# Attention outputs as positions by features turned by DMA in pairs, q and k of a block turned by one DMA, and groups of two

## The chip, the cores and the metric

The kernel runs on one core of one Trainium2 chip. The metric is device time in microseconds (us) of one execution. The core has a matrix engine (PE, with its weight loads listed as PEld), a vector engine (DVE), a scalar engine (ACT), GpSimd (POOL), and SyncE (SP), whose queue issues nearly all DMAs here; ACT's queue issues the stores of the output. Each engine works through its own queue in order.

## The reference, cut to what matters

Inputs q, k, v have shape 4 batches x 8 heads x 768 positions x 64 features. First comes linear attention with decay `lam` per head, in blocks along the positions:

```
intra = einsum('bhic,bhjc->bhij', qb, kb) * Dmask      # lam^(i-j) for j <= i
intra = einsum('bhij,bhjd->bhid', intra, vb)
inter = einsum('bhid,bhde->bhie', qb * lam_pow, kv_state)
out   = intra + inter
kv_state = lam_block * kv_state + einsum('bhsd,bhse->bhde', kb * rev_pow, vb)
```

The result, as 3072 tokens by 512 features (`x`), goes through two products: `h = x @ w_in` (512 x 2048), `g = h * sigmoid(h)`, and `g @ w_out` (2048 x 512), float32 at the end.

## The kernel before

Positions are taken 128 at a time: 24 blocks `u`, six for each batch (`blk` = 0 to 5 within a batch). Products are in bf16 with float32 sums in PSUM. For a block, `attention(u)` does this:

- q and k are loaded on SP's queue, scaled by powers of lam on DVE (`qs`, L325; `ks`, L390) and turned so that features lie on partitions. Blocks below `XB = 8` are turned on PE (`tr_ps`, L347, L398, L426). From block 8 on a DMA transpose on SP's queue does it: `kT` one block at a time (L409) and `qT` two blocks at a time (L337). For blocks 2 to 21 the positions of a pair of blocks are interleaved in q (`qf`, 512 KB for two blocks, L273); the four others (`plain`) load q on its own.
- `kTz` is k turned, put into a zero-padded tile by two copies (ACT or DVE, L230/L232).
- Scores `st_ps` (PE, L452, eight products), masked on DVE to `st_sb` (L461).
- The output `x_ps` (PE): eight products of `st_sb` with `vz`, v padded with zeros to two heads' width (L490), and for `blk > 0` four of the carried state `Xz` with q (L494). Here `vz` and `Xz` are the stationary operands, so the result lies as features x positions, 128 columns a product. ACT copies it into `xt` of the block's group (L230).
- The state: `d_ps` (PE, L521; L517 for the first blocks, where it is written in products of 64 columns), `y` on DVE, `Xz` and `Xf` on POOL (L235).

The blocks are put into groups for the two big products: `[0,1] [2,3] [4] [5] [6,7] [8,9] [10,11]` and then three groups of four. `first_product(g)` multiplies `w_in` (stationary) by the group's `xt` (moving, 128, 256 or 512 columns) into `h_ps` (L588); ACT makes `g` with SiLU (L597). `second_product(u)` multiplies `g` by `w_out`, 16 products of 512 columns for each block, into `o_ps` (L616; the last block's in halves, L655), which DVE copies to `o_sb` and ACT's queue stores.

Nothing waits on a clock. A planner (`Plan.run`) lists all steps with assumed costs, rings of buffers (`BUFS`) and priorities, and writes out each engine's instructions in the order that it finds. `pace(u)` and `at=` hold back steps of blocks 8 to 23 in this plan only: they set the order of the queues, not a wait on the chip. PE's queue so mixes the attention's short products with the big ones. In PE's order the attention of block 23 is followed by 76 products of L588 and 168 of L616, all with 512 columns, and the 32 of L655.

The order of both kernels' queues can be read without a run. Up to and with the 64 products of L588 for group `[6,7]` PE's two orders agree instruction by instruction; SP's agree up to the last load of `w_out`.

Of the kernel before, what the change touches and what calls it, by code (L numbers as in the profile page):

```python
# [7 lines left out]
F32 = mybir.dt.float32  # L8
# [92 lines left out]
def kernel(  # L101
# [10 lines left out]
    nc = tc.nc  # L112
# [10 lines left out]
    KO = DFF // 128  # L123
    HB = BLK // 2
    XB = 8
    WIDE = 4

    ctx.enter_context(tc.manual_schedule())
# [14 lines left out]
    def sb(o, name, shape, dtype, tag=None):  # L143
        return work.tile(shape, dtype, tag=tag or name, bufs=BUFS[tag or name], name=name)
# [80 lines left out]

    val = {}

    def copy(o, dst, src):
        if o["eng"] == "ACT":
            nc.scalar.activation(dst, src, AF.Copy)  # L230
        else:
            (nc.vector if o["eng"] == "DVE" else nc.gpsimd).tensor_copy(dst, src)  # L232
# [74 lines left out]
    def attention(u):  # L307
# [1 line left out]
        pr = at["v", u]  # L309


        if u in plain or u % 2 == 0:
            two = u not in plain
            lq = load["q", u]
            late = []
            if u >= 4:
                late = [plan.op({"NONE": 0.0}, [lq], lambda o: None, 0, after=2.0 if u >= 8 else 1.2, at=pace(u))]
# [13 lines left out]
            trs = []  # L331
            if u >= XB:
                n = len(halves)

                def fn(o):
                    val["qT", u] = sb(o, "qT", [128, 2, NP, BLK], BF16)
                    nc.sync.dma_start_transpose(  # L337
                        out=val["qT", u][:, 0:n].rearrange("p t a s -> p (t a) s"),
                        in_=val["qs", u][:, 0:n].rearrange("p t h d -> p (t h d)"))
                x = plan.op({"SP": 1.3 * n if n == 2 else 1.8}, [halves[-1]], fn, pr + 0.1, alloc=["qT"], frees=[(halves[0], "qs")])  # L340
                O["qT", u] = [x, plan.op({"NONE": 0.0}, [x], lambda o: None, 0, after=4.5)]
            for t in range(len(halves) if u < XB else 0):
# [9 lines left out]
            for t in range(len(halves) if u < XB else 0):  # L352
# [7 lines left out]
            if u < XB:  # L360
                O["qT", u] = evs
            if two:
                O["qT", u + 1] = O["qT", u]
        home = u if u in plain else u - u % 2

        def qT(p):
# [12 lines left out]
        if wide:  # L379
            def fn(o):  # L380
                val["ks", u] = kp[o["slots"]["kp"]]
                nc.vector.tensor_tensor(
                    val["ks", u].rearrange("p a b (c d) -> p a (b c) d", d=64)[:, :, 0:4:3, :],
                    val["kf", u].rearrange("p (a b) d -> p a b d", b=2),
                    lam_bwd.rearrange("p (a b) -> p a b", b=2)[:, :, :, None].to_broadcast([128, NP, 2, 64]),
                    op=AL.mult)
        else:
# [4 lines left out]
        ring_k = "kp" if wide else "ks"  # L392
        ks = plan.op({"DVE": 0.7}, [lk] + late, fn, pr, alloc=[ring_k], frees=[(lk, lk["tag"])])
        if wide:
            def fn(o):
                val["trk", u] = bank(o, "tr", [128, 2 * NP, BLK], BF16)
# [7 lines left out]
            kz = [plan.op({"ACT": 1.02, "DVE": 1.22}, [tk], fn, pr, alloc=["kTz"],  # L404
                          frees=[(tk, "bank"), (tk, "n_tr")])]
        elif u >= XB:
            def fn(o):
                val["kT", u] = sb(o, "kT", [128, NP, BLK], BF16)
                nc.sync.dma_start_transpose(  # L409
                    out=val["kT", u], in_=val["ks", u].rearrange("p h d -> p (h d)"))  # L410
            tk = plan.op({"SP": 1.8}, [ks], fn, pr, alloc=["kT"])
            landed = plan.op({"NONE": 0.0}, [tk], lambda o: None, 0, after=4.5)
            kz = []
            for hh in range(2):
                def fn(o, hh=hh):
                    if hh == 0:
                        val["kTz", u] = kTz[o["slots"]["kTz"]]
                    r = slice(64 * hh, 64 * hh + 64)
                    copy(o, val["kTz", u][r, :, hh, :], val["kT", u][r])
                kz.append(plan.op({"ACT": 0.59, "DVE": 0.35}, [tk, landed] + kz[:1], fn, pr,  # L420
                                  alloc=["kTz"] if hh == 0 else [], frees=[(tk, "kT")] if hh else []))
        else:
            def fn(o):
                val["trk", u] = bank(o, "tr", [128, NP, BLK], BF16)
# [57 lines left out]
        def fn(o):  # L482
# [4 lines left out]
            for p in range(NP):  # L487
# [7 lines left out]
        oo = plan.op({"PE": 0.0556 * (8 if blk == 0 else 12)}, masks + [vc] + prev_x + ([O["out", u - 1]] if u else []), fn, pr + 0.4,  # L495
                     alloc=["bank", "n_x"], frees=gives)
# [5 lines left out]
        O["xt", u] = plan.op({"ACT": 0.6, "DVE": 0.69}, [oo], fn, pr + 0.4, frees=[(oo, "bank"), (oo, "n_x")])  # L502

        last_st["frees"].append((kz[0], "kTz"))

# [5 lines left out]
        def fn(o):  # L511
            d = bank(o, "d", [128, NP, 64 if wide else 128], F32)
            val["d", u] = d
            for p in range(NP):
# [9 lines left out]
        dd = plan.op({"PE": 0.45 if wide else 0.225}, [ks, tk, vc], fn, pr + 0.35,  # L524
                     alloc=["bank", "n_d"], frees=[(ks, ring_k)])
        ys = []
        for hh in range(1 if wide else 2):
# [49 lines left out]
    def first_product(g):  # L577
# [4 lines left out]
        for m in range(KO // per):  # L582
            def fn(o, m=m):
                t = bank(o, "h", [128, per, nb * BLK], F32)
                val["h", g, m] = t
                for j in range(per):
                    for ko in range(KI):
                        nc.tensor.matmul(  # L588
                            t[:, j, :], lhsT=w_in_bf[:, ko, (m * per + j) * 128:(m * per + j + 1) * 128],
                            rhs=xts[g][:, ko, :], start=(ko == 0), stop=(ko == KI - 1))  # L590
# [138 lines left out]
```

## Time and profile before

| | us |
|---|---|
| median of 3 runs (lowest to highest) | 224.34 (224.01 to 224.50) |
| the profiled execution's own time | 223.49 |
| its span, first to last instruction | 221.8 |
| PE busy | 212.1 (96%) |
| PEld busy | 134.8 (61%) |
| DVE busy | 117.6 (53%) |
| ACT busy | 109.1 (49%) |
| POOL busy | 51.7 (23%) |
| SP's DMA queue (q1), packets' time as a share of 16 engines | 63.7%, 31.67 MB |
| ACT's DMA queue (q10) | 11.0%, 6.10 MB |

Busy times of different engines overlap. A matmul's duration in the profile holds the time that it spends in the array's pipeline; the next one starts well before it ends, so the distance from start to start tells what a product costs in a row of them. "x16" behind a piece is a count of instructions merged into it.

### The profile page before, as it was taken

To read this page: it belongs to the slowest core of one execution; us is meant where nothing else is said; L and a number is where in the kernel's file an instruction comes from. 1 tells how busy PE (TensorE), PEld (TensorE's weight loads), DVE (VectorE), ACT (ScalarE), POOL (GpSimd) and SP (SyncE) were. 2 spreads that over 40 slices of the span, in tenths; PEclk is the share of its full clock that TensorE was granted. 3 is DMA by queue.
4 is the path that set the end of the run, shared out by engine and by line. 5 is a ranking of instruction groups with operands and counts; after the bars stand their busy time and mean duration, and the time that the engine had idled before them with its cause. 6 is when DMAs were issued, how large, how long until landed. Compare 5 with 4: busy or idle time off the path is not lost.

```text
span 221.8 us, 4271 instructions
## 1 busy us (share of the span) xinstructions
PE 212.1 (96%) x1686; PEld 134.8 (61%) x1709; DVE 117.6 (53%) x198; ACT 109.1 (49%) x190; POOL 51.7 (23%) x71
## 2 busy tenths in 40 slices
PE   4889999999999999999999999999999999999994
PEld 1566699998745557978765656555554444444453
DVE  5676857878327786577788689753401120022121
ACT  5495488895712326785726773785351025500000
POOL 7364403035004051260444350442000000000000
PEclk9699999999999999999999999999999999999999
DMA  5999999999989979999999999910220422024332
GB/s 119 229 296 290 338 255 254 271 394 340 189 212 229 271 169 232 196 230 231 201 219 234 184 229 145 210 24 3 47 47 3 89 53 47 0 51 94 75 67 95
DMA packets 90243, 38.03 MB, mean 171 GB/s; under 512 B 72560, under 2 KB 83184, under 8 KB 90224
## 3 DMA queue, kind: packets, MB, share of 16 engines
q1 hardware_dynamic: 86448, 31.67, 63.7%
q10 hardware_dynamic: 3776, 6.10, 11.0%
q8 instruction: 13, 0.21, 0.4%
q14 instruction: 6, 0.05, 0.1%
HBM read 27.27 MB, written 6.29 MB: 151 GB/s over the span
## 4 chain that ended last, share of the span: by engine, by line
PE 87%; DMA 7%; DVE 2%; issue 1%; ACT 1%; SPq 1%; DVEq 0%
PE h_ps L588 37%; PE o_ps L616 36%; PE st_ps L452 4%; PE x_ps L490 4%; DMA wst<-in_moe_w_in_dram 4%; DMA qf<-in_q_dram 2%; PE x_ps L494 2%; PE d_ps L521 2%; PE o_ps L655 1%; DMA out_dram<-o_sb 1%; SPq L270 1%; PE tr_ps L347 1%; DVE w_in_bf L232 1%; DVE st_sb L461 1%; PE tr_ps L398 0%
## 5 line engine op out<-in xcount | busy, mean ns | idle before, releaser
L588 PE MATMUL h_ps<-xt,w_in_bf 128*128 128x256 bf16 (+2 forms) x634 | 89.9, 293 | 0.8 <-ACT xt L230 0.5
L616 PE MATMUL o_ps<-w_out_bf,g 128*128 128x512 bf16 x355 | 82.3, 379 | 0.7
L597 ACT ACTIVATE g<-h_ps 128x512 bf16<-128x512 f32 x96 | 56.5, 596 | 38.0 <-PE h_ps L588 22.3
L588 PEld LDWEIGHTS <-w_in_bf 128*128 128x128 bf16 x640 | 56.0, 98 | 23.1 <-PE x_ps L494 0.6
L616 PEld LDWEIGHTS <-g 128*128 128x128 bf16 x368 | 35.0, 98 | 37.6
L235 POOL TENSOR_TENSOR Xz<-y,lam_blk 64x256 bf16<-64x256 f32 x40 | 33.8, 845 | 99.2 <-DVE y L537 33.6
L232 DVE COPY o_sb<-o_ps 128x512 f32<-128x512 f32 (+2 forms) x24 | 15.9, 663 | 61.9 <-PE o_ps L616 58.8
L461 DVE TENSOR_TENSOR st_sb<-st_ps,mask 128x512 bf16<-128x512 f32 x48 | 32.0, 687 | 12.8 <-PE st_ps L452 12.6
L230 ACT ACTIVATE xt<-x_ps 128x512 bf16<-128x512 f32 x24 | 14.3, 595 | 26.1 <-PE x_ps L494 24.8
L325 DVE TENSOR_TENSOR qs<-qf,lam_fwd 128x512 bf16<-128x512 f32 x24 | 18.4, 780 | 3.5 <-DMA qf<-in_q_dram 3.4
L537 DVE TENSOR_TENSOR y<-d_ps,Xf 64x256 f32<-64x256 f32 (+1 forms) x29 | 12.2, 421 | 12.1 <-POOL Xf L235 8.7
L490 PE MATMUL x_ps<-st_sb,vz 128*128 128x128 bf16 x192 | 18.1, 219 | 0.3
L230 ACT ACTIVATE kTz<-kT 64x512 bf16<-64x512 bf16 x23 | 14.4, 626 | 7.8 <-DVE o_sb L232 6.0
L490 PEld LDWEIGHTS <-vz 128*128 128x128 bf16 x192 | 15.0, 98 | 5.3 <-issue 1.3
L452 PEld LDWEIGHTS <-kTz 128*128 128x128 bf16 x192 | 13.8, 100 | 6.6 <-ACT qT L230 0.6
L452 PE MATMUL st_ps<-qT,kTz 128*128 128x128 bf16 x192 | 17.4, 223 | 0.4
L390 DVE TENSOR_TENSOR ks<-kf,lam_bwd 128x512 bf16<-128x512 f32 x20 | 14.7, 734 | 0.3
L494 PE MATMUL x_ps<-qT,Xz 128*128 128x128 bf16 x80 | 14.5, 219 | 0.0
L235 POOL TENSOR_TENSOR Xf<-y,lam_blk 128x256 f32<-128x256 f32 x16 | 13.7, 853 | 1.3
L230 ACT ACTIVATE o_sb<-o_ps 128x512 f32<-128x512 f32 (+1 forms) x2 | 0.9, 437 | 26.0 <-DMA out_dram<-o_sb 25.7
L693 PE MATMUL warm_ps<-zeros 128*128 128x512 bf16 x25 | 8.8, 460 | 1.4 <-DVE pos L163 1.3
L230 ACT ACTIVATE vz<-vf 128x512 bf16<-128x512 f32 x11 | 6.9, 628 | 6.5 <-DVE y L537 3.2
(54 smaller groups left out, 98.0 us busy)
## 6 DMA issues: line engine op xcount, KB each, us to landing
kf<-in_k_dram SPq DMA_DIRECT2D x24, 256.0 KB, 5.1
vf<-in_v_dram SPq DMA_DIRECT2D x24, 256.0 KB, 4.9
qf<-in_q_dram SPq DMA_DIRECT2D x10, 512.0 KB, 6.7
out_dram<-o_sb ACTq DMA_DIRECT2D x40, 128.0 KB, 2.4
wst<-in_moe_w_in_dram SPq DMA_DIRECT2D x8, 512.0 KB, 6.2
wst<-in_moe_w_out_dram SPq DMA_DIRECT2D x8, 512.0 KB, 6.7
qf<-in_q_dram SPq DMA_DIRECT2D x4, 256.0 KB, 4.7
out_dram<-o_sb ACTq DMA_DIRECT2D x3, 256.0 KB, 2.5
```

What stands on the lines that cost most here:

```text
L230: nc.scalar.activation(dst, src, AF.Copy)
L232: (nc.vector if o["eng"] == "DVE" else nc.gpsimd).tensor_copy(dst, src)
L235: (nc.vector if o["eng"] == "DVE" else nc.gpsimd).tensor_tensor(dst, a, b, op=op)
L325: nc.vector.tensor_tensor(val["qs", u][:, t], src, lam_fwd[:, 1 + t if two else 0, :, None].to_broadcast([128, H, 64]), op=AL.mult)
L390: nc.vector.tensor_tensor(val["ks", u], val["kf", u], lam_bwd[:, :, None].to_broadcast([128, H, 64]), op=AL.mult)
L452: nc.tensor.matmul(val["st", u, half][:, i, :], lhsT=val["kTz", u][:, h // 2, h % 2, :], rhs=qT(h // 2), start=True, stop=True)
L461: nc.vector.tensor_tensor(val["st_sb", u, half], val["st", u, half], m[:, None, :].to_broadcast([128, 4, BLK]), op=AL.mult)
L490: nc.tensor.matmul(x[:, p, :], lhsT=vp[:, p, hh, :], rhs=val["st_sb", u, h // 4][:, h % 4, :], start=(hh == 0), stop=(hh == 1 and blk == 0))
L494: nc.tensor.matmul(x[:, p, :], lhsT=val["Xz", u][:, p, :], rhs=qT(p), start=False, stop=True)
L588: nc.tensor.matmul(t[:, j, :], lhsT=w_in_bf[:, ko, (m * per + j) * 128:(m * per + j + 1) * 128], rhs=xts[g][:, ko, :], start=(ko == 0), st ...
L597: nc.scalar.activation(t, val["h", g, m], AF.Silu)
L616: nc.tensor.matmul(val["o", u], lhsT=val["g", g, ko][:, i * BLK:(i + 1) * BLK], rhs=w_out_bf[:, ko, :], start=(ko == 0), stop=(ko == KO - 1))
```

## The change

1. From block 8 on no q is loaded in interleaved pairs: `plain` holds 0, 1 and 8 to 23. q and k of a block are loaded each on its own (256 KB), scaled into the two halves of one tile `qs` (`ks` is its second half), and turned by one DMA transpose into `qT`, which holds both. The ring `kT` is gone, `kf` has 6 buffers, `qs` 4, `ks` 2.
2. From block `XT = 10` on the output's operands change places: `st_sb` and `qT` are stationary, `vz` and `Xz` move. The result lies as positions x features; a product of `st_sb` has 64 columns, one of `Xz` 128. ACT or DVE copies it to a half of `x_sb`, and one DMA transpose on SP's queue turns both blocks of a pair into the pair's `xt`.
3. Groups are pairs from block 8 on, so L588 has 256 columns where it had 512 for blocks 12 to 23.
4. Stores of blocks 8 to 21 are one DMA a block instead of two. `pace` is 57 + 6.0 a block instead of 60 + 5.5.

```diff
+    XT = 10
-    BUFS = dict(kf=5, vf=5, qf=2, wst=6, qs=2, qT=5, ks=4, g=34, st_sb=6, o_sb=3, y=2, Xf=2,
-                kTz=3, vz=3, Xz=2, kp=3, kT=5)
+    BUFS = dict(kf=6, vf=5, qf=2, wst=6, qs=4, qT=5, ks=2, g=34, st_sb=6, o_sb=3, y=2, Xf=2,
+                kTz=3, vz=3, Xz=2, kp=3, x_sb=2)
...
-    groups = [[0, 1], [2, 3], [4], [5], [6, 7], [8, 9], [10, 11]] + [list(range(u, u + 4)) for u in range(12, NU, 4)]
+    groups = [[0, 1], [2, 3], [4], [5], [6, 7]] + [[u, u + 1] for u in range(8, NU, 2)]
...
-    xts = [const.tile([128, KI, len(us) * BLK], BF16, name=f"xt{g}") for g, us in enumerate(groups)]
+    xts = [const.tile([128, KI, len(us) * BLK] if us[0] < XT else [128, len(us), KI, BLK], BF16, name=f"xt{g}")
+           for g, us in enumerate(groups)]
-    plain = {0, 1, NU - 2, NU - 1}
+    plain = {0, 1} | set(range(XB, NU))
...
-        return 0.0 if u < 8 else 60.0 + 5.5 * (u - 8)
+        return 0.0 if u < 8 else 57.0 + 6.0 * (u - 8)
...
+            lq = load["q", u]
+            scaled = []
+            for t, (l, f, lam_t) in enumerate([(lq, "qf", lam_fwd[:, 0]), (lk, "kf", lam_bwd)]):
+                def fn(o, t=t, f=f, lam_t=lam_t):
+                    if t == 0:
+                        val["qs", u] = sb(o, "qs", [128, 2, H, 64], BF16)
+                        val["ks", u] = val["qs", u][:, 1]
+                    nc.vector.tensor_tensor(
+                        val["qs", u][:, t], val[f, u], lam_t[:, :, None].to_broadcast([128, H, 64]), op=AL.mult)
...
+                nc.sync.dma_start_transpose(
+                    out=val["qT", u].rearrange("p t a s -> p (t a) s"),
+                    in_=val["qs", u].rearrange("p t h d -> p (t h d)"))
+            turn = plan.op({"SP": 2.6}, scaled, fn, pr, alloc=["qT"])
+            landed = plan.op({"NONE": 0.0}, [turn], lambda o: None, 0, after=4.5)
...
-                nc.sync.dma_start_transpose(
-                    out=val["kT", u], in_=val["ks", u].rearrange("p h d -> p (h d)"))
-            tk = plan.op({"SP": 1.8}, [ks], fn, pr, alloc=["kT"])
...
+        if u >= XT:
+            def fn(o):
+                x = bank(o, "x", [128, H, 64], F32)
+                val["x", u] = x
+                for p in range(NP):
+                    if blk > 0:
+                        nc.tensor.matmul(x[:, 2 * p:2 * p + 2, :], lhsT=qT(p), rhs=val["Xz", u][:, p, :],
+                                         start=True, stop=False)
+                    for hh in range(2):
+                        h = 2 * p + hh
+                        nc.tensor.matmul(
+                            x[:, h, :], lhsT=val["st_sb", u, h // 4][:, h % 4, :], rhs=val["vz", u][:, p, 3 * hh, :],
+                            start=(blk == 0), stop=(blk == 0 or hh == 1))
...
+                copy(o, val["x_sb", u - u % 2][:, u % 2], val["x", u].rearrange("p h d -> p (h d)"))
...
+                    nc.sync.dma_start_transpose(
+                        out=xts[g][:, i - 1:i + 1].rearrange("p b a s -> p (b a) s"),
+                        in_=val["x_sb", u - 1].rearrange("p b f -> p (b f)"))
+                xT = plan.op({"SP": 2.6}, [O["xe", u - 1], xe], fn, pr + 0.4, frees=[(O["xe", u - 1], "x_sb")])
+                O["xt", u - 1] = O["xt", u] = plan.op({"NONE": 0.0}, [xT], lambda o: None, 0, after=4.5)
...
-                            rhs=xts[g][:, ko, :], start=(ko == 0), stop=(ko == KI - 1))
+                            rhs=xts[g][:, ko, :] if us[0] < XT else xts[g][:, :, ko, :], start=(ko == 0), stop=(ko == KI - 1))
```

More of the change, by code (lines that the diff above doesn't have):

```diff
@@ L309, in attention @@
         pr = at["v", u]
-        if u in plain or u % 2 == 0:
+        if u < XB and (u in plain or u % 2 == 0):
             two = u not in plain
@@ L316, in attention @@
             if u >= 4:
-                late = [plan.op({"NONE": 0.0}, [lq], lambda o: None, 0, after=2.0 if u >= 8 else 1.2, at=pace(u))]
+                late = [plan.op({"NONE": 0.0}, [lq], lambda o: None, 0, after=1.2)]
             halves = []
@@ L331, in attention @@
             trs = []
[L332 to L342, printed above, removed]
+            for t in range(len(halves)):
                 def fn(o, t=t):
@@ L351, in attention @@
             evs = []
-            for t in range(len(halves) if u < XB else 0):
+            for t in range(len(halves)):
                 def fn(o, t=t):
@@ L359, in attention @@
                                    frees=[(trs[0], "bank"), (trs[0], "n_tr")] if t == len(halves) - 1 else []))
-            if u < XB:
-                O["qT", u] = evs
+            O["qT", u] = evs
             if two:
-                O["qT", u + 1] = O["qT", u]
+                O["qT", u + 1] = evs
         home = u if u in plain else u - u % 2
@@ L386, in fn @@
                     op=AL.mult)
-        else:
+        elif u < XB:
             def fn(o):
@@ L391, in fn @@
                     val["ks", u], val["kf", u], lam_bwd[:, :, None].to_broadcast([128, H, 64]), op=AL.mult)
-        ring_k = "kp" if wide else "ks"
-        ks = plan.op({"DVE": 0.7}, [lk] + late, fn, pr, alloc=[ring_k], frees=[(lk, lk["tag"])])
+        else:
+            lq = load["q", u]
[7 more added lines that the diff above has]
+                        val["qs", u][:, t], val[f, u], lam_t[:, :, None].to_broadcast([128, H, 64]), op=AL.mult)
+                scaled.append(plan.op({"DVE": 0.7}, [l] + late + scaled[:1], fn, pr + 0.1 * (1 - t),
+                                      alloc=["qs"] if t == 0 else [], frees=[(l, l["tag"])]))
+            def fn(o):
+                val["qT", u] = sb(o, "qT", [128, 2, NP, BLK], BF16)
+                nc.sync.dma_start_transpose(
[3 more added lines that the diff above has]
+            landed = plan.op({"NONE": 0.0}, [turn], lambda o: None, 0, after=4.5)
+            O["qT", u] = [turn, landed]
+        ring_k = "kp" if wide else "ks" if u < XB else "qs"
+        if u < XB:
+            ks = plan.op({"DVE": 0.7}, [lk] + late, fn, pr, alloc=[ring_k], frees=[(lk, lk["tag"])])
+        else:
+            ks, tk = scaled[0], turn
         if wide:
@@ L406, in attention @@
         elif u >= XB:
-            def fn(o):
-                val["kT", u] = sb(o, "kT", [128, NP, BLK], BF16)
-                nc.sync.dma_start_transpose(
-                    out=val["kT", u], in_=val["ks", u].rearrange("p h d -> p (h d)"))
-            tk = plan.op({"SP": 1.8}, [ks], fn, pr, alloc=["kT"])
-            landed = plan.op({"NONE": 0.0}, [tk], lambda o: None, 0, after=4.5)
             kz = []
@@ L418, in fn @@
                     r = slice(64 * hh, 64 * hh + 64)
-                    copy(o, val["kTz", u][r, :, hh, :], val["kT", u][r])
+                    copy(o, val["kTz", u][r, :, hh, :], val["qT", u][r, 1])
                 kz.append(plan.op({"ACT": 0.59, "DVE": 0.35}, [tk, landed] + kz[:1], fn, pr,
-                                  alloc=["kTz"] if hh == 0 else [], frees=[(tk, "kT")] if hh else []))
+                                  alloc=["kTz"] if hh == 0 else []))
         else:
@@ L494, in fn @@
                     nc.tensor.matmul(x[:, p, :], lhsT=val["Xz", u][:, p, :], rhs=qT(p), start=False, stop=True)
-        oo = plan.op({"PE": 0.0556 * (8 if blk == 0 else 12)}, masks + [vc] + prev_x + ([O["out", u - 1]] if u else []), fn, pr + 0.4,
+        if u >= XT:
+            def fn(o):
+                x = bank(o, "x", [128, H, 64], F32)
[9 more added lines that the diff above has]
+                            start=(blk == 0), stop=(blk == 0 or hh == 1))
+        oo = plan.op({"PE": 0.029 * 8 + 0.0556 * (4 if blk else 0) if u >= XT else 0.0556 * (12 if blk else 8)}, masks + [vc] + prev_x + ([O["out", u - 1]] if u else []), fn, pr + 0.4,
                      alloc=["bank", "n_x"], frees=gives)
@@ L501, in fn @@
             copy(o, xts[g][:, :, i * BLK:(i + 1) * BLK], val["x", u])
-        O["xt", u] = plan.op({"ACT": 0.6, "DVE": 0.69}, [oo], fn, pr + 0.4, frees=[(oo, "bank"), (oo, "n_x")])
+        if u < XT:
+            O["xt", u] = plan.op({"ACT": 0.6, "DVE": 0.69}, [oo], fn, pr + 0.4, frees=[(oo, "bank"), (oo, "n_x")])
+        else:
+            def fn(o):
+                if u % 2 == 0:
+                    val["x_sb", u] = sb(o, "x_sb", [128, 2, H * 64], BF16)
+                copy(o, val["x_sb", u - u % 2][:, u % 2], val["x", u].rearrange("p h d -> p (h d)"))
+            xe = plan.op({"ACT": 0.6, "DVE": 0.69}, [oo], fn, pr + 0.4, alloc=["x_sb"] if u % 2 == 0 else [],
+                         frees=[(oo, "bank"), (oo, "n_x")])
+            O["xe", u] = xe
+            if u % 2:
+                def fn(o):
+                    g, i = group_of[u]
+                    nc.sync.dma_start_transpose(
[3 more added lines that the diff above has]
+                O["xt", u - 1] = O["xt", u] = plan.op({"NONE": 0.0}, [xT], lambda o: None, 0, after=4.5)
         last_st["frees"].append((kz[0], "kTz"))
@@ L523, in fn @@
                         rhs=val["vz", u][:, p, 0:4:3, :], start=True, stop=True)
-        dd = plan.op({"PE": 0.45 if wide else 0.225}, [ks, tk, vc], fn, pr + 0.35,
+        dd = plan.op({"PE": 0.45 if wide else 0.225}, [ks, tk, vc] + (scaled if u >= XB else []), fn, pr + 0.35,
                      alloc=["bank", "n_d"], frees=[(ks, ring_k)])
```

## The prediction

> **What bounds the kernel now.** I read the page first: busy times, the slices and the chain by line.
>
> ```profile
> PE 212.1 (96%) x1686; PEld 134.8 (61%) x1709; DVE 117.6 (53%) x198; ACT 109.1 (49%) x190; POOL 51.7 (23%) x71
> ...
> PE   4889999999999999999999999999999999999994
> ...
> DMA  5999999999989979999999999910220422024332
> ...
> PE 87%; DMA 7%; DVE 2%; issue 1%; ACT 1%; SPq 1%; DVEq 0%
> ```
>
> PE is full from the fifth slice to the last, and the chain that ends last runs over PE. The DMA engines are full too, but only up to slice 26 (144 us); DVE, ACT and POOL are far from it. A busy PE may still be slow, so I went on to the chain in order of time, for the distance from product to product:
>
> ```profile
> 38.62 1.75 PE h_ps L588 x16
> ...
> 101.57 0.45 PE x_ps L490 x8
> ...
> 144.47 1.73 PE h_ps L588 x8
> ...
> 159.05 2.59 PE o_ps L616 x12
> ...
> 216.75 0.44 DVE o_sb L232
> ```
>
> 1.75/16 = 109.4 ns for a product of 256 columns; 0.45/8 = 56 ns for 128; 1.73/8 = 216.2 ns for 512. These are the same everywhere, and from 52.66 us to 216.75 us the chain has nothing but PE pieces, save 0.05 us of "issue" here and there beside a missing record of one product. The windows say the same:
>
> ```profile
> 98.00:116.00 18.00, 17.84 (x174) 13.61 (x176) 13.93 (x25) 9.51 (x17) 5.32 (x7) 1.00 1.03 222
> 116.00:134.00 18.00, 17.89 (x128) 10.00 (x128) 13.81 (x24) 12.70 (x23) 7.43 (x9) 1.00 1.09 212
> ```
>
> The first number behind the length is PE: 17.84 and 17.89 of 18 us, clock 1.00. So in this stage time is the sum of PE's products, and a change counts by what it adds to that sum and by the waits that it brings into PE's queue, which runs in order.
>
> **The change part by part, on PE.** The trace of before holds products of 64 columns, in the first blocks' `d_ps`; the timeline of PE shows one row of them, and one of 128:
>
> ```profile
> 16.09 0.40 PE L517 MATMUL d_ps<-vz,kp 128*128 128x64 bf16 x8
> ...
> 101.40 0.61 PE L490 MATMUL x_ps<-st_sb,vz 128*128 128x128 bf16 x8
> ```
>
> A product of L517 lasts 0.193 us (median), one of L490 0.219, so the eight start (0.40 - 0.193)/7 = 29 ns and (0.61 - 0.219)/7 = 56 ns apart; two further rows of L517 give 28. I take 28.5. Each of these products has its own weight load, 98 ns long, and still they follow at 28.5 ns, so loads run beside one another and beside the products.
>
> - Output of blocks 10 to 23: eight products at 28.5 ns instead of 56: 8 x 27.5 = 0.22 us a block, 14 blocks: **-3.1 us**. The four of L494 only swap operands and keep 128 columns: 0.
> - Groups of two for blocks 12 to 23: 192 products of 512 columns (192 x 216.2 = 41.5 us) become 384 of 256 (384 x 109.4 = 42.0): **+0.5 us**. The moving operand is then two runs of 128 columns; L452 takes q in two runs of 64 now and costs 56 ns (0.45 us for eight in the chain), so nothing more.
>
> Sum on PE: -2.6 us, all of it on the path.
>
> Here a rule speaks against the change. The row is 56 ns from start to start at 128 columns and 28.5 at 64, with weight loads of 98 ns. The Trainium skill, page TensorE: Matmul & The Clock Gate, section Back-to-back issue gap, says that in a stream of load and product pairs both set the spacing, and gives some 81 ns at 128 columns. By that a shorter product behind a fresh load would gain little or nothing, and the sum would be about +0.5. The row decides: 56 is below 81, and halves with the columns.
>
> **What the change adds off PE, and who waits.**
>
> - *Stationary `st_sb`.* The weight load of an output product now waits for DVE's mask, where `vz` could be loaded ahead. Behind it on PE stands everything. In the chain no mask stands after 26 us, so the masks are done before PE comes to the output; I take 0. Bound: one load of 98 ns uncovered a block, 14 x 0.1 = +1.4.
> - *DVE, ACT, POOL.* Scalings stay 32 (0.69 us each), the copies of `kTz` and of `x_ps` (0.6) stay as many. ACT issues 14 stores instead of 28 (0.34 us instead of 0.47 + 0.6), which gives it some 10 us. None of them bounds: 0.
> - *q with k.* The turn of q now also waits for k's scaling, 0.69 us. Scores need both anyway: 0.
> - *DMA engines.* q alone moves the same bytes as in pairs, in pieces like `kf`. Seven pairs of outputs are turned: 14 x 0.131 MB = 1.84 MB more. Queue q1 needs 63.7% of 221.8 us = 141 us for 31.67 MB, 4.5 us a MB, so +8.2 us of all sixteen engines. `pace` spreads the 16 blocks over 96 us instead of 88, so 8 us more room is there, and after slice 26 the engines are nearly idle. I take 0.
> - *SP's queue.* It issues in order, and a transpose that waits for its data holds up the loads behind it:
>
> ```profile
> 105.87 2.02 SPq L337 DMA_TRANSPOSE qT<-qs  x1
> 108.00 3.56 SPq L409 DMA_TRANSPOSE kT<-ks  x2
> ...
> 117.19 3.51 SPq L337 DMA_TRANSPOSE qT<-qs  x1
> ```
>
> By the tile's own answer `qT` takes 1.21/2.02/3.51 us to issue (least, median, most; 1.21 is a single block) and lands 3.4/4.4/7.5 us after its start. Loads take 0.91 (`kf`), 0.88 (`vf`), 0.58 (q alone) and 1.38 (q in pairs) at the median. A pair of blocks costs SP 2.02 + 2 x 1.21 + 2 x 0.91 + 2 x 0.88 + 1.38 = 9.4 us before, and 3 x 2.02 + 2 x (0.91 + 0.88 + 0.58) = 10.8 after, with 12 us of pace. It fits, with little to spare.
>
> - *The output's turn.* From the last output product of a pair to the pair's first product of L588 there are now a copy (0.6), the wait in SP's queue and the landing (4.4, at most 7.5): 5.0 to 8.1 us plus the queue. I counted the cover in PE's order: it is least for `[22,23]`, 32 products of 256 columns and 32 of 512 (3.5 + 6.9 = 10.4 us), and 10.5 to 12.4 us for the six other pairs. So 0; without this cover it would cost 5 to 8 us a pair. After that turn PE still has 172 products, so the end of the kernel is its products and the same last store.
>
> Sum: -2.6. Against the profiled execution (223.49, span 221.8) that is 220.9. That execution is 0.85 below the median of the runs shown, so for the median: 224.34 - 2.6 = **221.7 us**.
>
> **The rivals.**
>
> *SP's queue becomes the bound: slower.* For: it has 10.8 of 12 us a pair, and a 2-block transpose took up to 3.51 us. With loads at the median it overflows at (12 - 4.74)/3 = 2.42 us a transpose; with loads at 0.57, as short as they run in the stage, at 2.86. At 3.0 it lags by 0.4 to 1.7 us a pair, over seven pairs 3 to 12 us, 7.5 in the middle; 10.4 - 8.1 = 2.3 of it is taken by the cover. Every further microsecond is one on PE: -2.6 + 7.5 - 2.3 = +2.6, **226.9 us**. Against: the long ones stand behind loads that filled the ring, and a queue that lags has an emptier ring, so the issues shorten.
>
> *Some turns land late.* The same steps, but only single ones: a pair's `xt` or a block's `qT` comes some tenths after PE's turn, or the 98 ns loads show. Seven to fourteen times 0.1 to 0.2 us: +0.7 to +2.3, **222.4 to 224.0**, about 223.2.
>
> *The short products don't gain.* If products of 64 columns cost 56 ns when the stationary operand is fresh from DVE, only the +0.5 stays: **224.8**. Against: three rows of L517, whose stationary `kp` came from DVE as well.
>
> **How the numbers follow.** Forecast (221.0 to 222.4) 0.70; single late turns 0.12; SP's queue 0.13; no gain 0.05. A measurement of this kernel can tell about 0.2% (0.45 us) from no change, so faster is below 223.9 and slower above 224.8. Faster: 0.70 and 0.09 of the late turns, 0.79. Same: 0.03 of these and 0.03 of the no gain, 0.06. Slower: 0.13 + 0.02 = 0.15. The range goes from 221.0 (runs differ by 0.3, and 0.4 us of the 0.85 between the pieces at 51.8 and 52.66 could close) to 224.0, the end of the late turns; above it are SP's queue and the no gain, 0.18.
>
> **What would show it.** Right: output products of 64 columns in rows of eight lines at 28 to 29 ns, 704 products of L588 with 256 columns at 109 ns, PE at 17.8 of 18 us in windows up to the end, and the last product 2.6 us sooner than 216.7. Wrong: idle time of PE before L588 put down to the landing of `xt`, or before L452 to `kTz` or `qT` with SP's transposes at 3 us; output products 56 ns apart; or DMA full past 160 us.

## The result, and the profile after

The changed kernel takes **221.35 us** (median of 4 runs, 220.87 to 221.97) against 224.42 (4 runs, 224.01 to 224.72) for the kernel before: ratio 0.9866, 95% interval 0.9836 to 0.9896. The forecast was 221.7 us. The profiled execution took 221.45 us with a span of 219.7 (before: 223.49 and 221.8).

Line numbers moved: L588 is now L630, L616 is L658, L655 is L697, L452 is L463, and the copies of L230 and L232 are L233 and L235. The new output products are L513 (`Xz`) and L517 (`st_sb`); the turns are L400 (q with k) and L540 (output).

From the page of the changed kernel: busy times, the slices of PE and of the DMA engines, and SP's queue.

```profile
PE 211.6 (96%) x1901; PEld 151.3 (69%) x1901; DVE 112.7 (51%) x189; ACT 113.4 (52%) x199; POOL 52.2 (24%) x71
...
PE   4899999999999999999999999999999999999993
...
DMA  5999998999999999999999999993911211021212
...
q1 hardware_dynamic: 100832, 33.50, 72.8%
```

PE is full from the third slice to the last but one, and the DMA engines now stay full up to slice 27 (148 us) and again in slice 29 (to 159 us), where before they were full up to slice 26. PE's busy time is of no use for the gain: it fell by 0.5 us only. Before, the trace holds 1686 products for 1709 weight loads, so 23 records are missing and count as idle; now all 1901 are there. The distances tell more. The chain in order of time (start, length, piece):

```profile
100.71 0.23 PE x_ps L517 x8
...
104.44 2.62 PE h_ps L630 x24
...
189.62 23.31 PE o_ps L658 x108
212.93 3.51 PE o_ps L697 x32
```

Eight output products take 0.23 us, 28 ns each, where eight of L490 took 0.45. A product of L630 costs 2.62/24 = 109 ns, one of L658 23.31/108 = 215.8: unchanged. The groups of PE by shape show the 64 and the 256 columns:

```profile
L630 PE MATMUL h_ps<-xt,w_in_bf 128*128 128x256 bf16 x704 | 82.9, 273 | 0.3 <-ACT xt L233 0.3
...
L517 PE MATMUL x_ps<-vz,st_sb 128*128 128x64 bf16 x112 | 7.6, 193 | 0.0
```

The windows of the two stretches shown of before (length, then PE, PEld, DVE, ACT, POOL busy, then clock, DMA share, GB/s):

```profile
98.00:116.00 18.00, 18.00 (x174) 13.47 (x173) 12.05 (x22) 9.86 (x17) 4.36 (x6) 1.00 1.13 225
116.00:134.00 18.00, 18.00 (x181) 14.14 (x179) 11.01 (x18) 12.64 (x24) 5.60 (x6) 1.00 1.18 227
```

After 56 us no product waits for more than 0.15 us. A single execution varies at its start: the first of the 64 products of group `[6,7]` began between 52.4 and 53.7 us in the profiled executions of this study (61.4 in that of cols128). I therefore measure a **stretch**: from the start of that product to the end of PE's last one, worked out from the trace. Up to its start PE's two orders agree. It was 165.80 us before (52.66 to 218.46) and is 163.30 now (53.12 to 216.42): **-2.51 us**, where the forecast's sum on PE was -2.6. A second execution of the changed kernel gave 163.30 again. Ratios leave out executions more than 1.5% above the fastest of their kernel, and two profiles below come from such an execution: that of cols128, at a granted clock of 0.75, gives no stretch, and that of split_qk (229.46 us, where the three others took 225.21 to 228.16) a longer one than usual.

### The profile page after: what moved, and what is told of

Read it like the earlier page. It is cut to its first block, busy times and chain, and to the rows that moved or that the text cites. A ratio compares the mean times of both kernels' runs of the same rounds, so it can differ in the third digit from the quotient of the medians.

```text
span 219.7 us, 4651 instructions
## 1 busy us (share of the span) xinstructions
PE 211.6 (96%) x1901; PEld 151.3 (69%) x1901; DVE 112.7 (51%) x189; ACT 113.4 (52%) x199; POOL 52.2 (24%) x71
## 3 DMA queue, kind: packets, MB, share of 16 engines
q1 hardware_dynamic: 100832, 33.50, 72.8%
## 4 chain that ended last, share of the span: by engine, by line
PE 92%; DMA 2%; ACT 2%; DVE 2%; issue 1%; SPq 0%; DVEq 0%
PE h_ps L630 38%; PE o_ps L658 36%; PE st_ps L463 5%; DMA qf<-in_q_dram 2%; PE x_ps L501 2%; PE d_ps L563 2%; PE o_ps L697 2%; PE warm_ps L735 2%; PE x_ps L517 1%; PE x_ps L513 1%; PE tr_ps L340 1%; DVE qs L328 1%; PE x_ps L505 1%; ACT xt L233 0%; ACT kTz L233 0%
## 5 line engine op out<-in xcount | busy, mean ns | idle before, releaser
L630 PE MATMUL h_ps<-xt,w_in_bf 128*128 128x256 bf16 (+1 forms) x832 | 90.9, 264 | 0.3 <-ACT xt L233 0.3
L658 PE MATMUL o_ps<-w_out_bf,g 128*128 128x512 bf16 x368 | 84.0, 379 | 0.0
L630 PEld LDWEIGHTS <-w_in_bf 128*128 128x128 bf16 x832 | 74.4, 98 | 8.5 <-PE warm_ps L735 0.6
L658 PEld LDWEIGHTS <-g 128*128 128x128 bf16 x368 | 34.9, 98 | 36.9
L235 DVE COPY o_sb<-o_ps 128x512 f32<-128x512 f32 (+2 forms) x23 | 15.2, 662 | 51.2 <-PE o_ps L658 48.8
L233 ACT ACTIVATE vz<-vf 128x512 bf16<-128x512 f32 x20 | 12.6, 630 | 14.7 <-DMA vf<-in_v_dram 12.4
L579 DVE TENSOR_TENSOR y<-d_ps,Xf 64x256 f32<-64x256 f32 (+1 forms) x29 | 12.2, 420 | 12.8 <-PE d_ps L563 5.6
L463 PE MATMUL st_ps<-qT,kTz 128*128 128x128 bf16 x192 | 17.7, 223 | 0.4
L463 PEld LDWEIGHTS <-kTz 128*128 128x128 bf16 x192 | 13.9, 100 | 5.2 <-ACT qT L233 0.6
L233 ACT ACTIVATE kTz<-qT 64x512 bf16<-64x512 bf16 x23 | 14.4, 624 | 2.8 <-DVE y L579 1.5
L233 ACT ACTIVATE o_sb<-o_ps 128x512 f32<-128x512 f32 (+1 forms) x3 | 1.5, 484 | 27.4 <-DVE o_sb L235 26.5
L233 ACT ACTIVATE x_sb<-x_ps 128x512 bf16<-128x512 f32 x14 | 8.3, 594 | 13.7 <-PE x_ps L517 13.7
L393 DVE TENSOR_TENSOR qs<-qf,lam_fwd 128x512 bf16<-128x512 f32 x16 | 11.6, 728 | 4.7 <-DMA qf<-in_q_dram 4.5
L393 DVE TENSOR_TENSOR qs<-kf,lam_bwd 128x512 bf16<-128x512 f32 x16 | 12.5, 782 | 1.1 <-DMA kf<-in_k_dram 1.0
L233 ACT ACTIVATE kTz<-tr_ps 64x512 bf16<-64x512 bf16 (+1 forms) x11 | 8.2, 747 | 2.8 <-PE tr_ps L415 2.6
L233 ACT ACTIVATE xt<-x_ps 128x512 bf16<-128x512 f32 x9 | 5.4, 595 | 5.5 <-PE st_ps L463 2.9
L501 PEld LDWEIGHTS <-vz 128*128 128x128 bf16 x80 | 6.2, 98 | 2.4 <-issue 1.3
```

The lines of the kernel that those rows point to most:

```text
L393: nc.vector.tensor_tensor(val["qs", u][:, t], val[f, u], lam_t[:, :, None].to_broadcast([128, H, 64]), op=AL.mult)
L463: nc.tensor.matmul(val["st", u, half][:, i, :], lhsT=val["kTz", u][:, h // 2, h % 2, :], rhs=qT(h // 2), start=True, stop=True)
L501: nc.tensor.matmul(x[:, p, :], lhsT=vp[:, p, hh, :], rhs=val["st_sb", u, h // 4][:, h % 4, :], start=(hh == 0), stop=(hh == 1 and blk == 0))
L579: nc.vector.tensor_tensor(val["y", u][r], d, val["Xf", u][r], op=AL.add)
L630: nc.tensor.matmul(t[:, j, :], lhsT=w_in_bf[:, ko, (m * per + j) * 128:(m * per + j + 1) * 128], rhs=xts[g][:, ko, :] if us[0] < XT else x ...
L658: nc.tensor.matmul(val["o", u], lhsT=val["g", g, ko][:, i * BLK:(i + 1) * BLK], rhs=w_out_bf[:, ko, :], start=(ko == 0), stop=(ko == KO - 1))
```

## The experiments

**Theory:** PE's sum of products is the bound; 64 columns in place of 128 bring the gain, the smaller groups give back 0.5 us, and DMA and SP's queue have room. **Rivals:** part of the gain comes from something else (q's new loads, the pace); or the queue is so near its end that what is given back is waits.

All ratios are to the kernel before, run alongside (its median 223.6 to 223.95).

| run | what it tries | median us | ratio [95%] | stretch us |
|---|---|---|---|---|
| after_again | the changed kernel | 221.51 | 0.9887 [0.9861, 0.9912] | 163.30 |
| cols128 | output products of 128 columns | 224.51 | 1.0019 [1.0005, 1.0032] | |
| xt24 | no turned outputs | 224.06 | 1.0013 [0.9998, 1.0029] | 166.28 |
| xt8 | turned outputs from block 8 | 221.20 | 0.9875 [0.9853, 0.9898] | 162.87 |
| fours | groups of four again | 221.36 | 0.9881 [0.9861, 0.9902] | 163.36 |
| pace55 | the old pace | 221.19 | 0.9894 [0.9871, 0.9918] | 163.30 |
| fours55 | groups of four, pace 57 + 5.5 | 220.62 | 0.9858 [0.9832, 0.9885] | 162.82 |
| turn_x2 | each output turned twice | 222.93 | 0.9950 [0.9925, 0.9975] | 164.99 |
| turn_x4 | each output turned four times | 233.35 | 1.0436 [1.0391, 1.0482] | 174.16 |
| split_qk | q and k turned by two DMAs | 227.04 | 1.0121 [1.0072, 1.0170] | 170.73 |
| split_told | the same, planner knows | 221.09 | 0.9902 [0.9871, 0.9934] | 163.30 |
| xt8_mid | turned outputs from block 8, pairs and fours | 220.41 | 0.9856 [0.9836, 0.9877] | 162.55 |

**1. The changed kernel once more**, no edit.

> The changed kernel once more, with more rounds, as the measure for the others. Theory A (the sum of PE's products: 64-column output products give -3.1 us, groups of two cost +0.5, everything else is hidden): 2.6 us below the kernel before, ratio 0.988. Theory B (a further part of the gain comes from elsewhere: fewer stores, q without pairs, another order of loads): 3 us or more below, ratio 0.986 or less, and a gain in the trace outside the stretch from the first product of group [6,7] to PE's last.

Measured: ratio 0.9887, which agrees with 0.9866 within the intervals, and the same stretch to 0.01 us. From here on a difference of 0.1 us in the stretch means something where PE does not wait, and the ratio bears it out where it exceeds some 0.25%.

**2. Only the width of the output products**, in the same place of every queue.

```diff
-    x[:, h, :], lhsT=val["st_sb", u, h // 4][:, h % 4, :], rhs=val["vz", u][:, p, 3 * hh, :],
-    start=(blk == 0), stop=(blk == 0 or hh == 1))
+    x[:, 2 * p:2 * p + 2, :], lhsT=val["st_sb", u, h // 4][:, h % 4, :],
+    rhs=val["vz", u][:, p, 2 * hh:2 * hh + 2, :],
+    start=(blk == 0 and hh == 0), stop=(hh == 1))
```

> Only the columns of the output products go back: each product of st_sb takes the zero-padded v of two heads, 128 columns, and the sum runs over both heads of a pair. The turned layout, the DMA transposes, the groups of two, the plan and the order of every queue stay. Theory A: 8 x 27.5 ns x 14 blocks come back, 3.1 us above the changed kernel, about 224.4 to 224.9, PE without idle time. Theory B: less than 3.1 comes back, the time stays clearly below the kernel before.

Measured: ratio 1.0019, against 0.9887 for the changed kernel run alongside: 1.3%, 3.0 us. With 128 columns, half of which only multiply the zeros of `vz`, the whole gain is gone and the kernel is a little slower than before, as the +0.5 of the groups has it.

**3. All of the change but the turned outputs.**

```diff
-    XT = 10
+    XT = 24
```

> XT = 24: no block's output is turned by DMA; outputs lie as features by positions again, 128 columns a product, and their seven DMA transposes are gone. q with k in one tile, plain q and groups of two stay. Theory A: the same as with 128 columns and the turns, 3.1 us above the changed kernel, since the turns are hidden: within 0.4 us of that run. Theory B (the turns by DMA cost something that PE waits for, or the new loading of q gains by itself): 0.5 us or more away from that run.

Measured: stretch 166.28, 0.48 above before and 2.99 above the changed kernel. Without the turned outputs the rest of the change (q with k, groups of two, pace) costs 0.48 us, the price of 384 products of 256 columns in place of 192 of 512 (0.50). The turned outputs bring 2.99; 112 products at 27.5 ns less are 3.08. So q with k, the stores and the pace together cost nothing and bring nothing.

**4. The turned outputs from block 8 on.**

```diff
-    XT = 10
+    XT = 8
```

> XT = 8: the outputs of blocks 8 and 9 are turned as well, an eighth DMA transpose; all else as in the changed kernel. Theory A: 2 blocks x 8 products x 27.5 ns = 0.44 us less on PE, the stretch from the first product of group [6,7] to PE's last 163.30 - 0.44 = 162.86 us, about 0.2% faster than the changed kernel. Rival: the first product of group [8,9] comes soon after its outputs in the order (2.2 us of other products in between in the changed kernel, with a copy of 0.6 us and no turn), and a landing of 3.1 us or more makes PE wait there or moves that group back in the order: no gain.

Measured: stretch 162.87, that is -0.43; 16 products at 27.5 ns are 0.44. The median (221.20 against 221.51) points the same way, but the intervals overlap.

**5. Groups of four, with the changed kernel's pace.**

```diff
-    groups = [[0, 1], [2, 3], [4], [5], [6, 7]] + [[u, u + 1] for u in range(8, NU, 2)]
+    groups = [[0, 1], [2, 3], [4], [5], [6, 7], [8, 9], [10, 11]] + [list(range(u, u + 4)) for u in range(12, NU, 4)]
```

> The changed kernel with the groups of before (three groups of four from block 12 on), still turned in pairs: L630 has 512 columns again for blocks 12 to 23. Theory A by columns alone: 192 products of 512 for 384 of 256, -0.5 us against the changed kernel, about 220.9. Rival: a group of four has to wait for the turn of its second pair, with fewer products in between, and PE idles before the first product of a group: same as the changed kernel or slower by 0.5 to 2 us, with idle time of PE before that line.

Measured: stretch 163.36, no gain. The 0.5 us of the products is there, but the new order puts one score group too early: the rival's wait is there, but at scores and not before the first product of a group. The timelines of PE and of DVE in this run:

```profile
125.42 0.22 PE L463 MATMUL st_ps<-qT,kTz 128*128 128x128 bf16 x1
126.01 0.34 PE L463 MATMUL st_ps<-qT,kTz 128*128 128x128 bf16 x3 [0.37 <-DVE kTz L235]
```

```profile
124.94 0.69 DVE L235 COPY o_sb<-o_ps 128x512 f32<-128x512 f32 x1 [1.03 <-PE o_ps L658]
125.67 0.29 DVE L235 COPY kTz<-qT 64x512 bf16<-64x512 bf16 x1
```

The second product starts 0.59 us after the first instead of 0.056: 0.54 us lost to DVE's copy of `kTz`. The turn was not late: it had landed at 121.10. The copy stood in DVE's queue behind one of `o_ps`, which waited for PE.

**6. The pace by itself, and with groups of four.**

```diff
-        return 0.0 if u < 8 else 57.0 + 6.0 * (u - 8)
+        return 0.0 if u < 8 else 60.0 + 5.5 * (u - 8)      # pace55
+        return 0.0 if u < 8 else 57.0 + 5.5 * (u - 8)      # fours55, with the groups of 5.
```

> The changed kernel with the pace of before, 60 + 5.5 a block. Theory A: another order of the queues, but PE still finds its data: stretch 163.3 us within 0.2, so the new pace brings nothing by itself. Rival: in the changed kernel the scores of block 16 follow their kTz by 0.6 us only; with blocks 0.5 us closer together that margin is gone and PE waits, 0.5 to 3 us slower.

> Groups of four with outputs turned in pairs, pace 57 + 5.5 a block. With groups of four and pace 57 + 6.0 the 0.48 us that 512 columns save were given back in one wait of 0.54 us before a product of L463 at 125 us. Theory A: that wait belongs to the order, and with this order it goes: stretch 163.30 - 0.48 = 162.82 us, 0.2% below the changed kernel. Rival: fours need the turn of a second pair before their first product and some wait of 0.5 us or more stays.

Measured: pace55 163.30, exactly as the changed kernel: the new pace by itself brings nothing. fours55 162.82, -0.48, with no wait of PE: groups of four bring their 0.5 us once the order leaves no late score. So the +0.5 that the change pays was no condition of turned outputs.

**7. Each output turn issued again**, once or three times more, into a tile that nobody reads any more.

```diff
                         in_=val["x_sb", u - 1].rearrange("p b f -> p (b f)"))
+                    for e in range(1):      # turn_x4: range(3)
+                        nc.sync.dma_start_transpose(
+                            out=kp[e].rearrange("p a b s -> p (a b) s"), in_=val["x_sb", u - 1].rearrange("p b f -> p (b f)"))
```

> Every DMA transpose of an output pair is issued twice, the second time into a tile that nothing reads any more; order of all queues as in the changed kernel. In the changed kernel an unhindered issue of a two-block transpose took 1.23 us, not the 2.02 of the forecast. Theory A with that: SP's queue has 3 x 1.23 + 6 x 0.57 = 7.1 of 12 us a pair unhindered, 8.3 with one more, and the sixteen DMA engines have some room: no change, within 0.2 us on the stretch of PE. Rival (the forecast's own slow case, 2.4 to 2.9 us a transpose as the limit): the queue is near its limit, 12.9 of 12 us by medians, and PE idles before L463 or L630, 1 to 5 us slower.

> The same with three transposes more a pair: unhindered 10.8 of 12 us on SP's queue, and the DMA engines get three times 0.26 MB more a pair. Theory A: here the limit is reached, by the DMA engines (landings follow each other by about 1.05 us for a load of 256 KB and 0.9 for a two-block transpose: 6.3 + 2.7 before and 6.3 + 5.4 = 11.7 us of 12 with three more, stores of the output not counted), so some idle time of PE shows, 1 to 8 us in all. Rival (there is far more room): no change, within 0.2 us.

Measured: +1.7 us of stretch with one more, in three waits (0.17, 0.97 and 0.53 us), where no change was expected, and +10.9 with three more, above the 1 to 8 us of its theory. Seven more turns already show, and 21 more cost over six times as much. In turn_x4 the longest wait stands at 125 us, for `kTz`. The windows of that run:

```profile
125.00:128.00 3.00, 0.23 (x1) 0.10 (x1) 0.44 (x2) 2.12 (x4) 0.00 (x0) 0.81 1.33 221
128.00:134.00 6.00, 5.83 (x20) 2.65 (x21) 1.38 (x2) 2.94 (x6) 0.00 (x0) 0.52 1.07 210
```

PE works 0.23 of 3 us, and then six microseconds at a clock of 0.52. The longer waits of both runs come about in one way: a load of q, k or v lands late, ACT or DVE stands before the step that needs it, and what PE needs comes behind that step in the same queue. In turn_x4 ACT waited 2.81 us for a load of v until 125.86, then made `g` and then the copy of `kTz`, though the turn of q and k had landed at 122.73; PE's score followed at 128.17. An extra turn takes both SP's queue and the DMA engines, and the order was made without it, so these two runs do not say which of the three makes the loads late; that stays open.

**8. q and k turned by two DMAs of one block**, in the place where the one of two stood.

```diff
-                nc.sync.dma_start_transpose(
-                    out=val["qT", u].rearrange("p t a s -> p (t a) s"),
-                    in_=val["qs", u].rearrange("p t h d -> p (t h d)"))
+                for t in range(2):
+                    nc.sync.dma_start_transpose(
+                        out=val["qT", u][:, t], in_=val["qs", u][:, t].rearrange("p h d -> p (h d)"))
```

> q and k of a block are turned by two DMA transposes of one block each instead of one of two; buffers, order and bytes as in the changed kernel. Theory A: SP's queue gets 2 x 1.21 us a pair more, 9.5 of 12 unhindered, and PE's stretch stays at 163.3 us within 0.2: turning q and k by one DMA brings no time by itself at this load. Rival: the queue lags and PE waits, 1 us or more slower, which would make the joint turn a condition of the gain.

Measured: ratio 1.0121, slower than before and, by the ratios, some 5 us above the changed kernel, where no change was expected. In the profiled execution the stretch is 7.4 us longer. There PE waits before scores at four places, 1.86 us at 82.4, 0.59 at 84.5, 2.02 at 127.0 and 1.28 at 157.9 (starts compared with the usual distance), 5.75 us together, and by the distances between the products from 85.1 to 88.7 some 1.7 us go to a lower clock: 7.4 by this count. The timeline of PE and the windows around the first:

```profile
81.74 1.03 PE L658 MATMUL o_ps<-w_out_bf,g 128*128 128x512 bf16 x4
84.47 0.23 PE L463 MATMUL st_ps<-qT,kTz 128*128 128x128 bf16 x1 [1.70 <-ACT kTz L233]
85.11 0.41 PE L463 MATMUL st_ps<-qT,kTz 128*128 128x128 bf16 x3 [0.42 <-ACT kTz L233]
85.32 1.91 PE L658 MATMUL o_ps<-w_out_bf,g 128*128 128x512 bf16 x4
```

```profile
82.00:85.00 3.00, 0.99 (x5) 0.25 (x3) 1.82 (x2) 2.31 (x4) 1.76 (x2) 1.00 1.29 218
85.00:89.00 4.00, 3.88 (x20) 2.43 (x21) 2.59 (x5) 0.69 (x2) 0.00 (x0) 0.57 0.90 230
```

The four products of 85.32 take 1.91 us where the same four at 81.74 took 1.03. None of the waits is for a turn that had yet to land. At 82.4 and 84.5 the scores of block 10 waited, whose turns had landed by 80.86, but the issue of two stores had held ACT until 82.60. At 127.0 it was block 16, with its turns landed by 121.52, and ACT's timeline shows what its copy of `kTz` stood behind:

```profile
126.73 0.63 ACT L233 ACTIVATE vz<-vf 128x512 bf16<-128x512 f32 x1 [3.30 <-DMA vf<-in_v_dram]
127.26 1.06 ACT L639 ACTIVATE g<-h_ps 128x512 bf16<-128x512 f32 x2
128.35 0.63 ACT L233 ACTIVATE kTz<-qT 64x512 bf16<-64x512 bf16 x1
```

The wait at 157.9 is for ACT's `g`, which stood behind a load of v as well (3.22 us). Is it that SP's queue has no room for 16 more DMAs, or that they come at a place that the order did not foresee?

**9. The same two DMAs, with their cost told to the planner.**

```diff
-            turn = plan.op({"SP": 2.6}, scaled, fn, pr, alloc=["qT"])
+            turn = plan.op({"SP": 3.6}, scaled, fn, pr, alloc=["qT"])
```

> q and k of a block turned by two DMA transposes again, but the planner is told what two cost (3.6 instead of 2.6 on SP's queue), so it writes another order of the queues. Theory A2 (the 7.4 us of waits with two transposes came from an order made for one: the scores stand in PE's queue for a moment at which kTz cannot be ready; the work on SP's queue itself, 9.5 of 12 us a pair unhindered, would fit): PE's stretch from the first product of group [6,7] comes back to 163.3 us within 1 us, some 222 us. Rival (SP's queue has no room for 1.2 us more a block, in whatever order): 3 us or more of waits before L463 stay.

Measured: ratio 0.9902, stretch 163.30, no wait. The 16 extra DMAs fit. What cost some 5 us, and 7.4 in the profiled execution, was an order written for one DMA: PE's queue takes the scores at the place where the planner believed `kTz` ready, and waits there, as ACT's queue waits before a load that the planner believed landed. So one DMA for q and k, taken by itself, brings nothing in time here; the matching order does.

**10. What the experiments point to:** turned outputs from block 8 on, pairs for blocks 8 to 15, fours for 16 to 23, and a slightly wider pace.

```diff
-    XT = 10
+    XT = 8
-    groups = [[0, 1], [2, 3], [4], [5], [6, 7]] + [[u, u + 1] for u in range(8, NU, 2)]
+    groups = [[0, 1], [2, 3], [4], [5], [6, 7]] + [[u, u + 1] for u in range(8, 16, 2)] + [list(range(u, u + 4)) for u in range(16, NU, 4)]
-        return 0.0 if u < 8 else 57.0 + 6.0 * (u - 8)
+        return 0.0 if u < 8 else 57.0 + 6.1 * (u - 8)
```

> The changed kernel with the turned output from block 8 on, the last eight blocks in groups of four (blocks 8 to 15 in pairs), and the pace at 57 + 6.1 per block, so that the groups of four find their transfers landed. Theory (PE's sum of products bounds as long as the order leaves the transfers time): blocks 8 and 9 give 2 x 8 x 27.5 ns = 0.44 us, and 128 products of 512 columns in place of 256 of 256 give 128 x (2 x 109.4 - 216.2) ns = 0.33 us; from the first product of group [6,7] to the last product 163.30 - 0.77 = 162.5 us, and about 0.8 us below the changed kernel: 220.5 us, ratio to the kernel before some 0.985. Rival (groups of four hold PE up, as the one wait of 0.54 us did with fours at the old pace): one or two waits of PE of 0.3 to 0.6 us before first products of scores, 162.9 to 163.4 us, and no gain that can be told from that of the turned output from block 8 on alone (ratio 0.9875).

Measured: 220.41 us, ratio 0.9856, stretch 162.55, 0.75 below the changed kernel as the sum has it. Its chain near the end:

```profile
185.54 13.81 PE h_ps L630 x64
...
211.44 3.51 PE o_ps L697 x32
```

64 products of 512 columns take 13.81 us, 215.8 ns each; 128 of 256 would take 14.0. It has the lowest median and the shortest stretch of all runs here; its interval overlaps those of fours55 and of the changed kernel. Its order is also the tightest of the runs without a wait: in block 13 the first score starts 0.17 us after the copies of `kTz` end (0.65 at the least in the changed kernel).

## Why the prediction was right, point by point

- **PE bounds, and only its sum counts.** Held: -2.51 in the stretch against -2.6. The two terms were measured apart: output products -2.99 (forecast -3.1; xt24 against the changed kernel), groups of two +0.48 (forecast +0.5; xt24 against before). fours55 and xt8 give -0.48 and -0.43 where the same prices have -0.50 and -0.44. The medians moved by 3.07 us in the first comparison and by 2.44 in the second, so it is the stretch that bears out the size, not the median.
- **Products of 64 columns at 28.5 ns behind fresh loads.** Held: 62 pairs of neighbours in L517 start 29 ns apart (median), and cols128 takes all of it back. The Trainium skill, page TensorE: Matmul & The Clock Gate, section Back-to-back issue gap, gives 81 ns at 128 columns and 131 at 512 for streams of loads and products; the traces of this case have 56 and 216, and the measurement decides. The formula that the section keeps for an isolated product, N/2.4 + 2.5 ns, gives 29, 56 and 216 at 64, 128 and 512 columns, which is what streams of loads and products do here.
- **Stationary `st_sb` at 0.** Held: each of the 50 rows of L517 that follow another line starts at that line's usual distance, at most 2 ns later. (The 0.0 us of idle time in the group's row would not show it, since a product's duration of 0.19 us covers a load of 98 ns.)
- **Where the last product ends.** The place was misread. 216.7 us in the chain of before is the end of the first half of L655, from where the chain follows a store; PE's last product ended at 218.46. From there to 216.42 are 2.04 us, and the changed kernel's profiled execution started its stretch 0.46 us later. The 2.5 is in the stretch, not in that pair of ends.
- **DMA engines.** The term was mis-sized, without effect on the time. The forecast was +8.2 us of all sixteen engines; q1 went from 63.7% of 221.8 to 72.8% of 219.7, 141.3 to 159.9, +18.7. xt24, which turns no output, has 67.3% of 222.2 = 149.5: so +8.3 come from q block by block, with the same bytes in more packets (93440 in place of 86448), which the forecast took as 0. The other 10.4 are the 1.84 MB of turns, 5.7 us a MB and not 4.5. ACT's queue, with fewer and larger stores, went the other way, from 11.0% to 8.1%, 6.6 us less. The engines were full in two slices more, to 159 us, just short of the 160 that the forecast named as a sign against it, and no wait of PE came of it.
- **SP's queue: 10.8 of 12 us a pair.** Mis-sized on the safe side. From the tile views of `qT` and of `x_sb` in the changed kernel (issue least/median/most in ns, first and last start; then the landing):

```profile
L400 SPq DMA_TRANSPOSE qT<-qs x16: 1232/2156/3865, 63.2 to 154.8; - x16
...
DMA to landing us min/median/max: 3.0/4.4/6.4
```

```profile
L540 SPq DMA_TRANSPOSE xt<-x_sb x7: 1232/1256/3283, 95.3 to 172.9; - x7
...
DMA to landing us min/median/max: 3.1/3.4/5.3
```

  The least issue of a DMA of two blocks is 1.23 us, hardly above that of one block (1.19, `kT` before), and the output turns have it as their median. The rest of the 2.02 that the forecast took as a price goes with earlier DMAs of the queue that are still under way. Of the 23 turns here, eight began with at most two of them not yet landed, and seven of these issued in 1.23 to 1.33 us (one in 2.21); the seven that began with four took 2.06 to 3.87. I read that as waiting for them, so the forecast counted waiting as work: 3 x 1.23 + 6 x 0.57 = 7.1 of 12 us is what a pair needs without it. This agrees with split_told, where 16 more DMAs cost nothing, and the rival of 226.9 us did not come: its condition, 2.42 to 2.86 us a turn, is at twice the least issue.
- **The rival's form was real, its path only in part.** split_qk and turn_x4 show what it priced, PE waiting before L463: all four waits of split_qk, and 6.4 of the 10.9 us of turn_x4. But in all of these waits over 0.4 us the turns had landed; late were loads and stores, and the copies of `kTz` or `g` stood behind them in ACT's and DVE's queues. And what decides is not SP's sum a pair: split_told issues the same DMAs as split_qk and loses nothing. It is the margin that the order leaves, most often between the copies of `kTz` and the first score. Worked out from the traces block by block for blocks 8 to 23, this is least 0.65 us in the changed kernel (block 16), 0.89 before, 0.53 in split_told, and negative in split_qk (2.0 us short in block 16).
- **Late single turns.** None in the changed kernel: q with k landed at least 4.0 us before the first score of its block, an output turn at least 3.8 us before the first product of its pair. The wait of 0.54 us in fours is not one either, since its turn had landed. The narrow place is behind the turns, at the copies: 0.65 us. (The sum of this rival was off as well: fourteen times 0.2 us are 2.8, not 2.3.)
- **The output's turn, covered by 10.4 us.** Held: it lands 3.1 to 5.3 us after its start, the cover came out at 10.2 to 12.2 us, and the only idle time before L630 (0.3 us in all) is put down to ACT's copies into `xt`, which the turned pairs do not have.

What was not tried: the turned outputs with q still in interleaved pairs. There q in pairs would have to be the stationary operand, and the kernel gives it no such form, so what plain q brings or costs was measured only without the turn (xt24).

## What to carry to other kernels

Where PE is full, price a change by the columns that it streams: zero padding in the moving operand costs as much as data, and swapping operands can drop it for a turn by DMA on a queue that has room. Price a DMA's issue by its least duration where the queue is free, and take the longer ones as a sign of earlier transfers under way. Where an order is planned ahead, a step that grows has to grow in the plan too: the same 16 DMAs cost some 5 us or nothing. And where a wait is put down to a copy, look at what stood before the copy in its own engine's queue: here it was a load of v, a store or another copy, not the turn that the copy reads.

## What the runs showed of the hardware

- A DMA transpose of two blocks (128 x 1024, bf16) issues in 1.23 us at the least and one of a single block in 1.19: the issue goes by DMA, hardly by size. Landing took 3.0 us at the least for two and 2.4 for one.
- Waits of PE can cost more than their length. After 1.86 + 0.59 us within 2.7 us (split_qk) the granted clock was 0.57 over the next 4 us, which cost 1.7 us, and after idle times of 1.1 + 2.4 us (turn_x4) 0.52 over the next 6. Waits of 2.0 and 1.3 us later in split_qk, one of 2.0 at 160 us in turn_x4 and one of 0.97 in turn_x2 left it at 1.00. The Trainium skill, same page, section HAM oscillation — how this bites in real kernels, puts the limit at gaps of about 3.4 us; here waits that add up to 2.4 us were enough once.
- Taking q block by block costs 8.3 us of all sixteen DMA engines more than taking it in pairs, for the same bytes (xt24 against before).
